# Attention, FFT mixing and FFN in one kernel: one PSUM bank per pair of heads, two in turn, and a new order table

## The chip, the cores and the metric

One core of a Trainium2 chip runs the whole program. The metric is the device time of one execution in microseconds (us); lower is better. TensorE (PE) multiplies, VectorE (DVE) and ScalarE (ACT) do the elementwise work, GpSimd (POOL) very little, and SyncE (SP) issues nearly all transfers.

## The reference

```python
def _attn_ref(q, k, v, cap):                       # (4, 12, 448, 64) each
    scores = np.matmul(q, k.transpose(0, 1, 3, 2)) / np.sqrt(q.shape[-1])
    scores = cap * np.tanh(scores / cap)
    scores = scores - np.max(scores, axis=-1, keepdims=True)
    attn = np.exp(scores)
    attn = attn / (np.sum(attn, axis=-1, keepdims=True) + 1e-09)
    return np.matmul(attn, v)

def _moe_ref(x, w_ch1, w_ch2):                     # x: (4, 448, 768), from attention
    mixed = np.real(np.fft.fft(np.fft.fft(x, axis=1), axis=2))
    u = x + mixed
    un = (u - mean(u)) / np.sqrt(var(u) + 1e-06)   # over the last axis
    return u + np.maximum(un @ w_ch1, 0.0) @ w_ch2 # 768 -> 3072 -> 768
```

## The kernel before

There are 4 batches of 12 heads; the heads go in 24 pairs, six to a batch, and two pairs share one set of q and k tiles. The kernel is a list of small steps. `ORDER` gives each step's place by hand: for each kind of step a list of numbers, by which all steps are sorted (`at`, `plan`). Each engine and the SP queue then run their instructions in that order, one after the other, and wait by semaphores where data or a buffer isn't ready.

For a pair of pairs there are seven *calls* t. `scores(t)` makes 448 queries x 128 rows of scores for two units in PSUM (tag "s", two tiles of two banks), in four 64 x 64 corners of PE. `tanh` moves them to SBUF (five buffers "a") and `exp` works there in place; both are on ACT. `weigh(u)`, two units per call, multiplies the exponentials with v and sums over the keys in PSUM: a pair has seven units, three times two of 128 keys of one head (units 6 or 8 matmuls each) and one of the last 64 keys of both heads. There the two heads lie in the upper and the lower 64 rows of PE, as two row tiles. v carries a column of ones, so one column of each block is the softmax denominator. The accumulator `av` is one tile of two PSUM banks, one bank for each head, and there is one such tile. When a pair's seven units are done, `denominators` and `normalise` on DVE divide and write `u`; the next pair's first matmul into `av` comes after that.

`transform` does the FFT part of a batch, after its six pairs: `fold_tokens`, `mirror`, `fold_features` (DVE), `stage1` (PE, `yps`), `combine` (ACT and DVE), `stage2` (PE, `pq`), `add_u`, `moments`, `rows`, `standardise` (DVE), `u_cols` (PE, `pt`), `u_copy`, `operand` (ACT), `operand_rest` and `residual` (DVE). Weights arrive as 64-bit words and are converted on DVE (`weights`, three steps of nine instructions in all for each half of a weight tile, from `raw` to `w`).

The FFN (`pieces`, step `product`) starts after the last `tanh`: 12 groups, in each for every batch `up` (36 matmuls, `ph`) and `down` (36 matmuls, `po`, each six added to `xc` by DVE at L821). In the first group `down_first` does the first two pieces of a batch with their adds at L845. `down` and `down_first` take their PSUM from tag "av", one tile of two banks (`both`, cut in two), and from tag "d", two tiles of one bank, in turn. Tag "d" also serves `yps`, `pq` and `pt`. From the second group on nothing but the FFN and the conversion of weights is left.

Of the kernel before, what the change touches and what calls it, by code (L numbers as in the profile page):

```python
# [65 lines left out]
PAD = 16, 16  # L66
# [35 lines left out]
        268, 267, 275, 302, 488, 487, 523, 524, 710, 727, 693, 702, 841, 846, 843, 850  # L102
    ],
    "combine": [
        237, 243, 238, 249, 436, 437, 449, 452, 649, 670, 659, 673, 830, 832, 826, 831
    ],
    "denominators": [
        44, 75, 104, 124, 155, 187, 216, 248, 286, 319, 342, 378, 426, 465, 504, 534, 566, 594, 641,
        686, 717, 748, 776, 793
    ],  # L110
    "exp": [
# [5 lines left out]
    ],  # L117
    "fetch": [
        8, 32, 43, 79, 145, 222, 299, 388, 479, 834, 854, 893, 921, 948
    ],  # L120
    "fold_features": [
        214, 228, 210, 223, 415, 419, 395, 407, 629, 637, 627, 634, 813, 815, 809, 811
    ],
    "fold_tokens": [
        149, 168, 186, 164, 196, 194, 261, 287, 367, 336, 382, 386, 498, 592, 554, 557, 607, 608, 698,
        749, 775, 767, 803, 804
# [5 lines left out]
        133, 110, 66, 212  # L132
    ],
    "load_k": [
        0, 28, 50, 37, 91, 106, 128, 161, 177, 245, 258, 264, 315, 376, 372, 438, 494, 477, 515, 581,
        590, 650, 699, 737
    ],
    "load_q": [
        1, 15, 11, 25, 49, 59, 80, 76, 115, 152, 165, 176, 202, 213, 234, 280, 262, 308, 334, 348, 359,
        397, 402, 433, 490, 503, 502, 548, 539, 570, 632, 666, 646, 704, 725, 736  # L140
    ],
    "load_v": [
# [3 lines left out]
    ],  # L146
    "mirror": [
        199, 203, 387, 393, 609, 619, 805, 806
    ],
    "moments": [  # L150
        273, 312, 307, 311, 495, 510, 544, 532, 729, 733, 759, 762, 852, 855, 853, 856
    ],
    "normalise": [
        46, 82, 109, 127, 157, 190, 219, 251, 290, 321, 343, 381, 431, 470, 514, 541, 569, 600, 647,
        690, 722, 751, 777, 798
    ],
    "operand": [
        421, 425, 453, 454, 442, 507, 695, 639, 677, 715, 678, 799, 848, 816, 828, 900, 901, 906, 909,
        923, 916, 907, 920, 927
    ],  # L160
    "operand_rest": [
        458, 430, 486, 469, 456, 537, 720, 652, 680, 723, 763, 833, 886, 822, 887, 902, 910, 911, 912,
        929, 925, 938, 937, 941
    ],
    "product": [
# [3 lines left out]
    ],  # L169
    "residual": [  # L170
        605, 642, 800, 837, 866, 897, 932, 919, 934, 956, 953, 963
    ],
    "row": [
        584, 752, 908, 946
    ],
    "rows": [
        341, 561, 783, 867
    ],
    "rows_cols": [
        346, 564, 794, 875  # L180
    ],
    "rows_copy": [
        355, 598, 795, 880
    ],
    "rows_out": [
        405, 418, 466, 416, 621, 661, 657, 675, 810, 861, 840, 851, 888, 922, 928, 939
    ],
    "scales": [
        4
    ],  # L190
    "scores": [
# [5 lines left out]
    ],  # L197
    "stage1": [
        233, 242, 236, 246, 434, 435, 443, 446, 640, 658, 651, 664, 827, 829, 824, 821
    ],  # L200
    "stage2": [
        259, 254, 269, 291, 473, 472, 505, 511, 709, 716, 684, 687, 838, 845, 839, 849
    ],
    "standardise": [
        363, 354, 347, 368, 567, 576, 583, 580, 790, 789, 791, 786, 876, 879, 883, 874
    ],
    "tanh": [
# [5 lines left out]
    ],  # L213
    "u_cols": [
        374, 375, 391, 392, 409, 414, 599, 597, 616, 620, 628, 633, 796, 802, 814, 808, 862, 869, 884,
        889, 891, 896, 892, 899
    ],
    "u_copy": [
        385, 390, 401, 412, 424, 428, 610, 614, 622, 625, 631, 636, 801, 807, 817, 819, 865, 873, 885,
        890, 895, 898, 904, 905  # L220
    ],
    "warmup": [
        2
    ],
    "weigh": [
# [9 lines left out]
    ],  # L235
    "weights": [
        9, 24, 27, 40, 67, 84, 87, 96, 97, 113, 122, 141, 180, 230, 235, 326, 349, 380, 422, 444, 445,
        556, 586, 648, 663, 689, 825, 872, 878, 894, 915, 930, 940, 944, 947, 950, 959, 962, 964, 966,
        968, 970
    ],  # L240
}


ENGINES = {
    "u_copy": "AAAA",
# [34 lines left out]
def attention_fft_ffn(  # L280
# [60 lines left out]


    vt = new([P, 2, NC, D + 1], F32, "vt", 1, "vt")
    nc.gpsimd.memset(vt[:, :, :, :1], 1.0)

    qk = {}

# [719 lines left out]
```

## Time and profile before

| | before |
|---|---|
| median of 3 runs | 911.3 us (910.24 to 913.85) |
| the profiled execution's own time | 913.63 us |
| its span in the trace | 910.8 us |
| granted TensorE clock | 1.0 |

The span runs from the first to the last instruction that the trace holds; the execution's own time has some 2.8 us more around it. Times in the trace are counted from the span's start. PE shows as busy for 98% of the span, DVE for 80% and ACT for 36%.

### The profile page before, as it was taken

How to read it: one execution, taken by the hardware profiler on the slowest of the kernel's cores; microseconds unless marked ns; L12 is line 12 of the kernel's file. 1: busy time of each engine (PE TensorE's matmuls, PEld its weight loads, DVE VectorE, ACT ScalarE, POOL GpSimd, SP SyncE). 2: the span in 40 equal slices, each digit the busy share in tenths (PEclk: the TensorE clock that was granted, in tenths of full speed). 3: DMA queues.
4: the chain of work that ended last, by engine and by line, in shares of the span. 5: the costliest groups of instructions: out<-in, count | busy, mean ns of one | idle time of the engine just before them, and what ended most of it. 6: DMA issues, size and time to landing. Idle time of an engine off the chain costs nothing.

```text
span 910.8 us, 17992 instructions
## 1 busy us (share of the span) xinstructions
PE 892.0 (98%) x7452; PEld 784.8 (86%) x7452; DVE 728.4 (80%) x1540; ACT 327.1 (36%) x503; POOL 9.7 (1%) x19
## 2 busy tenths in 40 slices
PE   8899999999989999999999999999999999999998
PEld 4566676778889999999999999999999999999998
DVE  4689999999889787878878788787787877878633
ACT  7989999961502212122221221212212221222200
POOL 0000001000000000000000000000000000000000
PEclk9999999999999999999999999999999999999999
DMA  7653535210202121211212211111211111221033
GB/s 212 172 139 104 135 91 164 66 47 1 74 4 84 53 63 55 72 59 53 63 53 63 65 57 53 53 53 53 67 57 53 53 52 53 54 68 53 18 120 123
DMA packets 50465, 66.60 MB, mean 73 GB/s; under 512 B 25408, under 2 KB 36560, under 8 KB 50384
## 3 DMA queue, kind: packets, MB, share of 16 engines
q1 hardware_dynamic: 50096, 65.13, 24.6%
q8 instruction: 58, 0.95, 0.4%
q10 hardware_dynamic: 288, 0.33, 0.1%
q14 instruction: 23, 0.19, 0.1%
HBM read 59.92 MB, written 5.52 MB: 72 GB/s over the span
## 4 chain that ended last, share of the span: by engine, by line
PE 90%; DVE 7%; issue 1%; ACT 1%; POOL 0%; DVEq 0%; POOLq 0%
PE po L813 37%; PE ph L778 37%; PE av L439 7%; PE s L410 6%; PE pq L561 2%; DVE u L477 1%; PE yps L533 1%; DVE xc L768 1%; DVE tf L502 1%; DVE tf L496 1%; DVE ff L515 0%; DVE y L553 0%; PE warm L351 0%; DVE xs L329 0%; PE pt L644 0%
## 5 line engine op out<-in xcount | busy, mean ns | idle before, releaser
L778 PE MATMUL ph<-xs,w 128*128 128x448 f32 x1728 | 353.3, 362 | 0.0
L813 PE MATMUL po<-hh,w 128*128 128x448 f32 (+1 forms) x1686 | 343.7, 362 | 3.6 <-DVE xc L845 3.6
L778 PEld LDWEIGHTS ph<-xs,w 128*128 128x128 f32 x1728 | 323.4, 187 | 21.9 <-issue 0.3
L813 PEld LDWEIGHTS po<-hh,w 128*128 128x128 f32 x1686 | 314.3, 187 | 27.1 <-DVE xc L845 5.1
L821 DVE TENSOR_TENSOR xc<-xc,po 128x448 f32<-128x448 f32 (+1 forms) x281 | 172.2, 616 | 40.3 <-PE po L813 40.2
L790 DVE SCALAR_TENSOR_TENSOR hh<-ph,hh 128x448 fp32r<-128x448 f32 x96 | 59.9, 624 | 87.3 <-ACT hh L789 86.6
L691 ACT ACTIVATE wt<-raw 128x384 f32<-128x384 f32 x84 | 46.6, 555 | 230.5 <-DVE w L725 230.5
L789 ACT ACTIVATE hh<-ph 128x448 fp32r<-128x448 f32 x96 | 52.3, 544 | 187.1 <-PE ph L778 187.1
L439 PEld LDWEIGHTS av<-vt,a 128*64 128x64 f32 (+1 forms) x2688 | 76.7, 137 | 33.7 <-issue 17.2
L439 PE MATMUL av<-vt,a 128*64 128x65 f32 (+1 forms) x2688 | 82.5, 223 | 8.0 <-issue 3.7
L420 ACT ACTIVATE a<-s,tscale 128x896 f32<-128x896 f32 x84 | 82.5, 1005 | 11.8 <-PE s L410 9.7
L324 ACT CAST w<-wt 128x384 fp32r<-128x384 f32 x84 | 42.8, 510 | 117.8 <-DVE wt L700 117.8
L423 ACT ACTIVATE a<-a,capt 128x896 f32<-128x896 f32 x84 | 83.6, 1039 | 0.4
L410 PE MATMUL s<-q,k 64*64 64x448 f32 x672 | 78.5, 560 | 1.5 <-ACT a L420 1.5
L700 DVE SCALAR_TENSOR_TENSOR wt<-wt 128x384 f32<-128x384 f32 x96 | 53.6, 558 | 9.2
L697 DVE SCALAR_TENSOR_TENSOR wt<-raw,wt 128x384 uint32<-128x384 uint32 x96 | 53.7, 559 | 3.3
L725 DVE TENSOR_TENSOR w<-wt 128x384 fp32r<-128x384 f32 x96 | 53.6, 558 | 3.3
L719 DVE SCALAR_TENSOR_TENSOR wt<-raw,wt 128x384 f32<-128x384 uint32 x96 | 53.5, 557 | 2.9
L329 DVE TENSOR_TENSOR wt<-wt,w 128x384 f32<-128x384 f32 x96 | 52.8, 550 | 0.0
L410 PEld LDWEIGHTS s<-q,k 64*64 64x64 f32 x672 | 23.0, 134 | 21.4 <-issue 9.6
L694 DVE TENSOR_SCALAR wt<-raw 128x384 uint32<-128x384 uint32 x96 | 34.1, 355 | 1.1
L716 DVE TENSOR_SCALAR wt<-wt 128x384 uint32<-128x384 uint32 x96 | 33.9, 354 | 0.5
(65 smaller groups left out, 367.7 us busy)
## 6 DMA issues: line engine op xcount, KB each, us to landing
raw<-w2r SPq DMA_DIRECT2D x48, 384.0 KB
raw<-w1r SPq DMA_DIRECT2D x48, 384.0 KB
q<-qr SPq DMA_DIRECT2D x35, 224.5 KB
outT<-xc SPq DMA_DIRECT2D x23, 224.0 KB
k<-kr SPq DMA_DIRECT2D x12, 256.0 KB
vt<-vr SPq DMA_DIRECT2D x24, 128.0 KB
vt<-vr SPq DMA_DIRECT2D x24, 96.0 KB
k<-kr SPq DMA_DIRECT2D x12, 192.0 KB
```

The lines of the kernel that those rows point to most:

```text
L410: nc.tensor.matmul(ps_t[t][h * D : (h + 1) * D, n, :SQ], kt[q, k][rows, k0, h], qk[q, x][rows, :SQ], start=True, stop=True,)
L420: nc.scalar.activation(a_t[t], ps_t.pop(t)[:, :, :SQ], AF.Tanh, scale=tscale)
L423: nc.scalar.activation(a_t[t], a_t[t], AF.Exp, scale=capt)
L439: nc.tensor.matmul(pa_t[p][half * D : (half + 1) * D, j, g * (D + 1) : g * (D + 1) + w], a_t[t][rows, n, q : q + D], vt[rows, p % 2].rearr ...
L697: nc.vector.scalar_tensor_tensor(tu, hi.bitcast(U32), 0xC0000000, tu, op0=ALU.bitwise_and, op1=ALU.bitwise_or)
L700: nc.vector.scalar_tensor_tensor(t, w, HI_MIN, t, op0=ALU.is_ge, op1=mul)
L719: nc.vector.scalar_tensor_tensor(w, lo, 2.0**-52, w, op0=mul, op1=mul)
L725: nc.vector.tensor_tensor(ws[c][1][:, sl], t, w, op=add)
L778: nc.tensor.matmul(ph[:, :S], w_[:, dc * P : (dc + 1) * P], x_, start=(k_ == 0), stop=(k_ == 3 * NDC - 1),)
L790: nc.vector.scalar_tensor_tensor(hh[:, 1], ph[:, :S], 0.0, f32(hh[:, 0]), op0=ALU.max, op1=sub)
L813: nc.tensor.matmul(po[:, q0:q1], w_[:, dc * P : (dc + 1) * P], hh[:, x_, q0:q1], start=(k_ == 0), stop=(k_ == 3 * GF - 1),)
L821: nc.vector.tensor_tensor(ac[:, q0:q1], ac[:, q0:q1], po[:, q0:q1], op=add)
```

## The change

Blocks of 65 columns (64 of v and the column of ones, now the last) of a pair lie side by side in one PSUM bank: three for each head and one for the last 64 queries of both, seven in all. There are two such banks, for even and odd pairs in turn. The last 64 keys of the two pairs that share q and k form the two units in the middle (u = 6 and 7 of 14): unit 6 is the first head of both pairs, unit 7 the second, and each pair has a row tile of its own and writes its own bank. So an even pair ends with unit 7 and an odd pair begins with unit 6. With this the third copy of the queries falls away: two `load_q` in place of three per pair of pairs. `down` and `down_first` take single banks of tag "av" and tag "d" in turn. All lists of `ORDER` are new; the host arrays follow.

```diff
-PAD = 16, 16
+PAD = 24, 16
...
     "denominators": [
-        44, 75, 104, 124, 155, 187, 216, 248, 286, 319, 342, 378, 426, 465, 504, 534, 566, 594, 641,
+        65, 77, 115, 131, 165, 178, 222, 265, 300, 315, 359, 371, 423, 472, 508, 530, 572, 587, 644,
...
-    nc.gpsimd.memset(vt[:, :, :, :1], 1.0)
+    nc.gpsimd.memset(vt[:, :, :, D:], 1.0)
...
-        (nc.scalar if q == 0 and i == 0 else nc.sync).dma_start(qk[q, i], qr[q, i])
+        (nc.scalar if q == 0 and i == 0 else nc.sync).dma_start(qk[q, i], qr[q, i // 2])
...
-        nc.sync.dma_start(vt[:, p % 2, n0:n1, 1:], vr[p // NP, PAIRS[p % NP], :, n0:n1])
+        nc.sync.dma_start(vt[:, p % 2, n0:n1, :D], vr[p // NP, p % NP, :, n0:n1])
...
-                x = (2 * n if n == h else 1) if i == 3 else 2 * (i > 3)
+                x = 2 * (h if i == 3 else i > 3)
...
         p, head, c = chunk(u)
-        if u % NC == 0:
-            pa_t[p] = psum.tile([P, 2, 512], F32, tag="av", bufs=1, name="av")
-        i = 6 if head is None else 2 * c + head
-        first, last = ((0, 1), (6, 6)) if p % 2 == 0 else ((0, 0), (6, 6))
-
-        def tile(j, g, half, rows, n, i):
+        if u % (2 * NC) in (0, NC - 1):
+            pa_t[u // NC + (u % NC > 0)] = psum.tile([P, 512], F32, tag="av", name="av")
+
+        def tile(p, j, g, half, rows, n, i, start):
+            block = 3 * j + g if g < 3 else 6
             q = (2 * g + half) * D if g < 3 else 6 * D
-            w = D + 1 + int(g == 2 and c == 0 and half != j)
             nc.tensor.matmul(
-                pa_t[p][half * D : (half + 1) * D, j, g * (D + 1) : g * (D + 1) + w],
+                pa_t[p][half * D : (half + 1) * D, block * (D + 1) : (block + 1) * (D + 1)],
                 a_t[t][rows, n, q : q + D],
-                vt[rows, p % 2].rearrange("k n c -> k (n c)")[:, i * (D + 1) : i * (D + 1) + w],
-                start=u % NC == first[j] and g == 0,
-                stop=u % NC == last[j] and g == 3,
+                vt[rows, n if i == NC - 1 else p % 2, i],
+                start=start,
+                stop=False,
                 skip_group_check=True,
             )
 
+        if head is None:
+            p -= p % 2
+            for g in range(3):
+                for h in range(2):
+                    for half in range(2):
+                        tile(p + h, n, g, half, slice(h * D, (h + 1) * D), n, NC - 1, h == 1 and n == g == 0)
+            if n == 1:
+                for j in range(2):
+                    for h in range(2):
+                        tile(p + h, j, 3, j, slice(h * D, (h + 1) * D), j, NC - 1, False)
+            return
         for g in range(3):
-            for j in (0, 1) if head is None else (head,):
-                rows = slice(P) if head is not None else slice(j * D, (j + 1) * D)
-                for half in range(2):
-                    tile(j, g, half, rows, n, i)
-        for j in range(2):
-            if head is None:
-                tile(j, 3, j, slice(j * D, (j + 1) * D), n, i)
-            elif head == 1:
-                tile(j, 3, j, slice(P), n - 1 + j, i - 1 + j)
+            for half in range(2):
+                tile(p, head, g, half, slice(P), n, 2 * c + head, u % (2 * NC) == g == 0)
+        if head == 1:
+            for j in range(2):
+                tile(p, j, 3, j, slice(P), n - 1 + j, 2 * c + j, False)
...
-        pa = pa_t[p][:, :, : 4 * (D + 1)].rearrange("q j (g c) -> q j g c", g=4)
-        den = den_t[p] = new([P, 2, 4, 1], F32, "den", 2, "den")
-        nc.vector.tensor_scalar_add(den, pa[:, :, :, :1], guard)
+        pa = pa_t[p][:, : 7 * (D + 1)].rearrange("q (i c) -> q i c", i=7)
+        den = den_t[p] = new([P, 7, 1], F32, "den", 2, "den")
+        nc.vector.tensor_scalar_add(den, pa[:, :, D:], guard)
...
-        def part(out, rows, j, g):
-            x = pa[rows, j, g]
-            nc.vector.tensor_tensor(out, x, den[rows, j, g].to_broadcast(x.shape), op=mul)
-
-        part(u[D:FOLD, :, 3], slice(FOLD, P), slice(2), 2)
-        nc.vector.memset(den[FOLD:, :, 2], 0.0)
+        def part(out, rows, i):
+            x = pa[rows, i]
+            nc.vector.tensor_tensor(out, x, den[rows, i].to_broadcast(x.shape), op=mul)
+
+        part(u[D:FOLD, :, 3], slice(FOLD, P), slice(2, 6, 3))
+        nc.vector.memset(den[FOLD:, 2:6:3], 0.0)
         for j in range(2):
-            part(u[:D, j, 3], slice(j * D, (j + 1) * D), j, 3)
-        part(u[:, :, :3], slice(P), slice(2), slice(3))
+            part(u[:D, j, 3], slice(j * D, (j + 1) * D), 6)
+        nc.vector.tensor_tensor(
+            u[:, :, :3],
+            pa[:, :6].rearrange("q (j g) c -> q j g c", j=2),
+            den[:, :6].rearrange("q (j g) c -> q j g c", j=2).to_broadcast([P, 2, 3, D]),
+            op=mul,
+        )
...
-        both = yield from down_first(b) if g == 0 else ()
+        if g == 0:
+            yield from down_first(b)
         for dc in range(2 * (g == 0), NDC):
 
-            if dc % 2:
-                po = psum.tile([P, 512], F32, tag="d", name="po")
-            else:
-                if dc % 4 == 0:
-                    both = psum.tile([P, 2, 512], F32, tag="av", bufs=1, name="po")
-                po = both[:, dc % 4 // 2]
+            po = psum.tile([P, 512], F32, tag=("av", "d")[dc % 2], name="po")
...
-        both = psum.tile([P, 2, 512], F32, tag="av", bufs=1, name="po")
-        po = both[:, 0], psum.tile([P, 512], F32, tag="d", name="po")
+        po = [psum.tile([P, 512], F32, tag=tag, name="po") for tag in ("av", "d")]
...
-            at(load_v, p, i, needs=[("weigh", u) for u in units(p - 2)])
+            at(load_v, p, i, needs=[("weigh", 7 * p - 8 + n) for n in range(2 - p % 2)] if p > 1 else [])
...
-                at(denominators, p, needs=[("weigh", 7 * p + 6), ("guards",)] + ([("denominators", p - 1)] if p else []))
+                at(denominators, p, needs=[("weigh", 7 * p + 7 - p % 2), ("guards",)] + ([("denominators", p - 1)] if p else []))
```

How the order moves instructions is shown at three places. First VectorE, the rows up to the first denominators (`den`; `w` and `wt` are a converted weight and its scratch). Before:

```order
L725 TENSOR_TENSOR w_177<-wt 128x384
L693 TENSOR_SCALAR wt<-raw 128x384
L694 TENSOR_SCALAR wt<-raw 128x384
L697 SCALAR_TENSOR_TENSOR wt<-raw,wt 128x384
L700 SCALAR_TENSOR_TENSOR wt<-wt 128x384
L466 TENSOR_SCALAR den<-av,guard 128x8
L467 RECIPROCAL den<-den 128x8
```

After:

```order
L735 TENSOR_TENSOR w_193<-wt 128x384
L703 TENSOR_SCALAR wt<-raw 128x384
L704 TENSOR_SCALAR wt<-raw 128x384
L707 SCALAR_TENSOR_TENSOR wt<-raw,wt 128x384
L710 SCALAR_TENSOR_TENSOR wt<-wt 128x384
L726 TENSOR_SCALAR wt<-wt 128x384
L326 CAST w_308<-wt 128x384
L729 SCALAR_TENSOR_TENSOR wt<-raw,wt 128x384
L471 TENSOR_SCALAR den<-av,guard 128x7
L472 RECIPROCAL den<-den 128x7
```

The first denominators now stand behind the third conversion's first seven instructions, 12 conversion instructions later than before.

Second TensorE, at the change from the second pair to the third (`av` with its number is the accumulator, `a` the exponentials, `s` the scores). Before:

```order
L439 MATMUL av_284<-vt_92,a_273 64x65 x8
L410 MATMUL s_383<-q_323,k_219 64x448 x4
L410 MATMUL s_392<-q_323,k_219 64x448 x4
L439 MATMUL av_402<-vt_92,a_313 64x65 x5
L439 MATMUL av_402<-vt_92,a_313 64x66
L439 MATMUL av_402<-vt_92,a_313 64x65 x4
```

After:

```order
L437 MATMUL av_259<-vt_92,a_246 64x65 x14
L437 MATMUL av_259<-vt_92,a_244 64x65 x14
L437 MATMUL av_385<-vt_92,a_325 64x65 x14
L410 MATMUL s_405<-q_220,k_323 64x448 x4
L437 MATMUL av_385<-vt_92,a_321 64x65 x14
L410 MATMUL s_430<-q_220,k_323 64x448 x4
```

Before, the third pair's tile `av_402` starts behind two calls of scores; now its bank `av_385` follows the second pair's last unit directly. The shared units stand earlier, as alternating rows of `av_157` and `av_259`:

```order
L410 MATMUL s_248<-q_169,k_222 64x448 x4
L437 MATMUL av_157<-vt_92,a_167 64x65 x2
L437 MATMUL av_259<-vt_92,a_167 64x65 x2
L437 MATMUL av_157<-vt_92,a_167 64x65 x2
L437 MATMUL av_259<-vt_92,a_167 64x65 x2
```

Third TensorE, in the first FFN group, from `down_first` of a late batch to the third and fourth piece of the same `down` (`po` with its number is the PSUM tile). Before:

```order
L836 MATMUL po_3787<-hh_3745,w2_177 128x448 x3
L836 MATMUL po_3788<-hh_3745,w2_177 128x448 x3
L836 MATMUL po_3787<-hh_3783,w2_452 128x448 x3
L836 MATMUL po_3788<-hh_3783,w2_452 128x448 x3
L813 MATMUL po_3787<-hh_3745,w2_177 128x448 x3
L813 MATMUL po_3787<-hh_3783,w2_452 128x448 x3
L813 MATMUL po_3817<-hh_3745,w2_177 128x448 x3
L813 MATMUL po_3817<-hh_3783,w2_452 128x448 x3
```

After:

```order
L841 MATMUL po_3751<-hh_3718,w2_193 128x448 x3
L841 MATMUL po_3752<-hh_3718,w2_193 128x448 x3
L841 MATMUL po_3751<-hh_3745,w2_308 128x448 x3
L841 MATMUL po_3752<-hh_3745,w2_308 128x448 x3
L819 MATMUL po_3782<-hh_3718,w2_193 128x448 x3
L819 MATMUL po_3782<-hh_3745,w2_308 128x448 x3
L819 MATMUL po_3792<-hh_3718,w2_193 128x448 x3
L819 MATMUL po_3792<-hh_3745,w2_308 128x448 x3
```

Before, the third piece goes into the second bank of the tile whose first bank took the first piece (`po_3787`); now it has a bank of its own (`po_3782`). In the changed order the first `yps` of batch 0 stands behind 28 calls of `scores` and 406 matmuls of `weigh` (7.25 pairs), where it stood behind 30 calls and 426 (7.61 pairs); for batch 1 it is 48 calls and 692 (12.36 pairs) against 50 and 728 (13).

## Rows read from the trace of the kernel before

**Rows 1.** The page: span, and busy time, share and instructions of PE.

```profile
span 910.8 us, 17992 instructions
PE 892.0 (98%) x7452; PEld 784.8 (86%) x7452; DVE 728.4 (80%) x1540; ACT 327.1 (36%) x503; POOL 9.7 (1%) x19
```

**Rows 2.** Windows: stretch, busy us and instructions by engine, clock, DMA share, GB/s.

```profile
7.30:62.00 54.70, 49.22 (x1016) 29.75 (x1008) 35.49 (x99) 50.31 (x55) 0.00 (x0) 1.00 0.63 173
62.00:196.00 134.00, 129.50 (x2777) 92.57 (x2774) 126.79 (x336) 122.12 (x149) 6.22 (x8) 1.00 0.37 102
196.00:275.00 79.00, 75.37 (x478) 66.42 (x477) 73.35 (x151) 22.90 (x44) 1.27 (x2) 1.00 0.12 37
275.00:910.80 635.80, 632.78 (x3168) 592.22 (x3166) 491.10 (x947) 130.09 (x253) 0.00 (x0) 1.00 0.20 61
```

**Rows 3.** Chain that ended last, in time order: start us, us, what.

```profile
113.89 1.95 PE yps L533 x32
...
118.29 1.66 PE s L410 x16
119.95 2.12 PE pq L561 x32
...
145.39 3.32 PE av L439 x112
...
237.20 2.32 PE pt L644 x24
```

**Rows 4.** Timeline at the first and last change of pair: start, us, what.

```profile
17.47 1.04 DVE L477 TENSOR_TENSOR u<-av,den 64x64 f32<-64x64 f32 x3
...
18.62 0.59 PE L439 MATMUL av<-vt,a 64*64 64x65 f32 x25 [0.54 <-PE s L410]
...
191.59 1.04 DVE L477 TENSOR_TENSOR u<-av,den 64x64 f32<-64x64 f32 x3
...
192.74 0.65 PE L439 MATMUL av<-vt,a 64*64 64x65 f32 x27 [1.38 <-issue]
```

**Rows 5.** Waits of DVE, 7 to 62 and 62 to 200: us, times, longest.

```profile
DVE den L466 <- PE av L439: 16.7, 6, 5.6
...
DVE y L553 <- ACT yh L324: 0.9, 1, 0.9
DVE den L466 <- PE av L439: 0.7, 3, 0.4
```

**Rows 6.** Waits of ACT, 7.3 to 62 us.

```profile
ACT a L420 <- PE s L410: 5.7, 5, 1.6
```

**Rows 7.** Waits of PE from 196 us on, and the timeline at the third wait.

```profile
PE po L813 <- DVE xc L845: 3.6, 4, 1.4
...
250.33 2.08 DVE L768 TENSOR_TENSOR xc<-xc,dev 128x896 f32<-128x896 f32 x2
252.33 1.14 DVE L845 TENSOR_TENSOR xc<-xc,po 128x448 f32<-128x448 f32 x2
...
253.00 1.28 PE L813 MATMUL po<-hh,w 128*128 128x448 f32 x5 [1.43 <-DVE xc L845]
```

**Rows 8.** Timeline of DVE: first and last of the nine instructions of a conversion.

```profile
6.46 0.36 DVE L693 TENSOR_SCALAR wt<-raw 128x384 uint32<-128x384 uint32 x1 [0.58 <-DMA raw<-w2r]
...
9.91 0.56 DVE L725 TENSOR_TENSOR w<-wt 128x384 fp32r<-128x384 f32 x1
```

**Rows 9.** Timeline of DVE: denominators of the eighth and the last pair.

```profile
69.46 0.23 DVE L466 TENSOR_SCALAR den<-av,guard 128x8 f32<-128x8 f32 x1
...
196.08 0.23 DVE L466 TENSOR_SCALAR den<-av,guard 128x8 f32<-128x8 f32 x1
```

**Rows 10.** Groups of DVE by form, 0 to 200 us: busy us, mean ns, idle before.

```profile
L585 DVE TENSOR_TENSOR u<-u,pq 128x384 f32<-128x384 f32 x24 | 11.7, 547 | 0.1
```

**Rows 11.** Timeline at the first `yps` of batch 0.

```profile
63.36 0.63 DVE L515 TENSOR_TENSOR ff<-tf 128x194 f32<-128x194 f32 x2
...
64.21 1.92 PE L533 MATMUL yps<-seqT,ff 128*64 128x128 f32 x32
```

More of the change, by code (lines that the diff above doesn't have):

```diff
@@ L131 @@
     "load_constant": [
-        133, 110, 66, 212
+        197, 148, 47, 185
     ],
     "load_k": [
-        0, 28, 50, 37, 91, 106, 128, 161, 177, 245, 258, 264, 315, 376, 372, 438, 494, 477, 515, 581,
-        590, 650, 699, 737
+        1, 16, 37, 59, 73, 71, 128, 174, 204, 216, 278, 277, 283, 377, 416, 417, 464, 498, 507, 519,
+        564, 608, 697, 731
     ],
     "load_q": [
-        1, 15, 11, 25, 49, 59, 80, 76, 115, 152, 165, 176, 202, 213, 234, 280, 262, 308, 334, 348, 359,
-        397, 402, 433, 490, 503, 502, 548, 539, 570, 632, 666, 646, 704, 725, 736
+        2, 11, 23, 36, 93, 124, 157, 146, 191, 232, 257, 295, 308, 361, 395, 459, 490, 492, 542, 586,
@@ L155 @@
-        690, 722, 751, 777, 798
+        72, 91, 121, 141, 177, 181, 246, 268, 306, 318, 370, 374, 429, 480, 520, 532, 583, 591, 657,
+        703, 741, 758, 786, 791
     ],
     "operand": [
-        421, 425, 453, 454, 442, 507, 695, 639, 677, 715, 678, 799, 848, 816, 828, 900, 901, 906, 909,
-        923, 916, 907, 920, 927
+        441, 489, 390, 458, 457, 408, 601, 624, 626, 675, 637, 800, 797, 877, 813, 886, 890, 894, 891,
+        893, 902, 919, 918, 912
     ],
     "operand_rest": [
-        458, 430, 486, 469, 456, 537, 720, 652, 680, 723, 763, 833, 886, 822, 887, 902, 910, 911, 912,
@@ L163 @@
-        929, 925, 938, 937, 941
+        531, 588, 559, 593, 539, 411, 667, 690, 816, 743, 824, 811, 868, 879, 829, 888, 892, 896, 914,
+        916, 917, 926, 925, 930
     ],
     "product": [
[3 rows of a table removed]
[3 rows of a table added]
     ],
     "residual": [
-        605, 642, 800, 837, 866, 897, 932, 919, 934, 956, 953, 963
+        640, 668, 642, 771, 858, 882, 898, 905, 921, 941, 949, 953
     ],
     "row": [
-        584, 752, 908, 946
+        578, 654, 867, 935
     ],
     "rows": [
-        341, 561, 783, 867
+        319, 533, 746, 847
@@ L178 @@
     ],
     "rows_cols": [
-        346, 564, 794, 875
+        347, 548, 761, 863
     ],
     "rows_copy": [
-        355, 598, 795, 880
+        360, 550, 776, 866
     ],
     "rows_out": [
-        405, 418, 466, 416, 621, 661, 657, 675, 810, 861, 840, 851, 888, 922, 928, 939
+        387, 406, 528, 476, 561, 615, 584, 605, 789, 790, 857, 820, 872, 933, 911, 899
     ],
     "scales": [
-        4
+        3
     ],
     "scores": [
[5 rows of a table removed]
[5 rows of a table added]
     ],
     "stage1": [
-        233, 242, 236, 246, 434, 435, 443, 446, 640, 658, 651, 664, 827, 829, 824, 821
+        219, 230, 224, 237, 407, 403, 428, 433, 645, 656, 639, 661, 815, 814, 817, 819
@@ L216 @@
-        889, 891, 896, 892, 899
+        362, 363, 368, 378, 384, 397, 582, 585, 606, 627, 611, 635, 767, 794, 805, 803, 826, 856, 870,
+        874, 878, 876, 880, 885
     ],
     "u_copy": [
-        385, 390, 401, 412, 424, 428, 610, 614, 622, 625, 631, 636, 801, 807, 817, 819, 865, 873, 885,
-        890, 895, 898, 904, 905
+        367, 369, 382, 386, 389, 401, 590, 609, 623, 628, 631, 643, 774, 801, 810, 812, 831, 859, 871,
+        875, 883, 884, 895, 897
     ],
     "warmup": [
-        2
+        0
@@ L846, in down_first @@
             yield
-        return both
     def pieces():
@@ L899, in prepare @@
         for i in range(2):
-            at(load_v, p, i, needs=[("weigh", u) for u in units(p - 2)])
+            at(load_v, p, i, needs=[("weigh", 7 * p - 8 + n) for n in range(2 - p % 2)] if p > 1 else [])
             if p % 2 == 0:
-                for x in (0,) if i == 0 else (1, 2):
-                    t0, t1 = ((0, 4), (3, 4), (3, 7))[x]
+                x = 2 * i
+                if 1:
+                    t0, t1 = ((0, 4), (), (3, 7))[x]
                     at(load_q, p // 2, x, needs=[("scores", 7 * (p // 2 - 1) + t) for t in range(t0, t1)] if p else [])
@@ L909, in attend @@
         pairs = sorted({u // 7 for u in (2 * t, 2 * t + 1)})
-        at(scores, t, needs=[("load_q", t // NC, x) for x in ((0, 1, 2) if t % NC == 3 else (2 * (t % NC > 3),))] + [("load_k", t // NC, int(t % NC >= KT[1]))])
+        at(scores, t, needs=[("load_q", t // NC, x) for x in ((0, 2) if t % NC == 3 else (2 * (t % NC > 3),))] + [("load_k", t // NC, int(t % NC >= KT[1]))])
         at(tanh, t, needs=[("scores", t), ("scales",)])
@@ L1036 @@
     for j in range(2):
-        kr[..., 3, j * D : (j + 1) * D] = kj[:, :, j, :, 3 * P :]
+        kr[..., 3, j * D : (j + 1) * D] = kj[:, j, ..., 3 * P :]
+    vj = v.reshape(B, NP, 2, S, D)[:, PAIRS]
     vr = np.empty((B, NP, P, NC, D), np.float32)
     for j in range(2):
-        vr[:, :, :, j:6:2] = v[:, j::2, : 3 * P].reshape(B, NP, 3, P, D).transpose(0, 1, 3, 2, 4)
-        vr[:, :, j * D : (j + 1) * D, 6] = v[:, j::2, 3 * P :]
+        vr[:, :, :, j:6:2] = vj[:, :, j, : 3 * P].reshape(B, NP, 3, P, D).transpose(0, 1, 3, 2, 4)
+        vr[:, j::2, :, 6] = vj[:, :, j, 3 * P :].reshape(B, NP // 2, P, D)
     arrays = {
         "qr": np.concatenate(
-            [qr.reshape(B * NP // 2, 3, P, SQ), np.broadcast_to(np.float32(cap), (B * NP // 2, 3, P, 1))], axis=3
+            [qj.reshape(B * NP // 2, 2, P, SQ), np.broadcast_to(np.float32(cap), (B * NP // 2, 2, P, 1))], axis=3
         ),
```

34 lines of the change are left out of this document (16 added, 18 removed), and 60 rows, old and new, of the table ORDER.

## The prediction, on record before the changed kernel ran

> **What bounds the kernel now.** I read the stretches first, then the chain of waits, then single places. The page has PE busy for 892 us of a span of 910.8 [rows 1]. By stretch the kernel falls in two [rows 2]: from 275 us on there are 3168 matmuls in 635.8 us, 0.2007 us each, with no gap, so nothing the change does can shorten that part; it can only start sooner. Before 275 us PE is also nearly always marked busy, but a marked PE is not a full one, so I rebuilt its work from back-to-back groups [rows 3]: 16 score matmuls take 1.66 us (0.83 us for one call of `scores`), a pair's 112 `weigh` matmuls 3.32, 32 `yps` 1.95, 32 `pq` 2.12, 24 `pt` 2.32. Up to the last `weigh` at 196.0 us that is 84 x 0.83 + 24 x 3.32 + 6 x 1.95 + 6 x 2.12 + 2 x 2.32 = 178.4 us. The scores begin at 5.5 us, so 190.5 us were available and **12.1 us of PE were lost** in the attention part.
>
> Where: at the change of pair. The one accumulator tile is read by `normalise`, and the next pair's first matmul follows it. At the first change `normalise` ends at 17.47 + 1.04 = 18.51 and PE starts at 18.62; at the last it ends at 192.63 and PE starts at 192.74 after 1.38 us idle [rows 4]. Of the 23 changes 17 look like this (start within 0.26 us of the end of `normalise`); at the other six PE had enough other work in front.
>
> The loss has a second side. DVE stood 16.7 us before 62 us with a denominator at the head of its queue, waiting for PE; from 62 to 200 us it waited 0.7 us for that and 0.9 us for ACT [rows 5] and was busy 126.8 of 134.0 us [rows 2]. So DVE idles early and sets the pace later: the early idle is what could pay for the later part. ACT waited 5.7 us for scores between 7.3 and 62 us [rows 6]; its busy time from 7.3 to 196 us is 50.3 + 122.1 = 172.4 us [rows 2], so it could not end the attention before about 180 us. The granted clock is 1.00 in every stretch [rows 2].
>
> After 196 us PE waits at four places only, 3.6 us together, all at L813 for the add of L845 [rows 7]. There `down` wants the second half of the two-bank tile while the add still reads the first half: DVE does two `residual` steps at 250.33 and the add at 252.33, and PE starts at 253.00.
>
> **The change, part by part.**
>
> *One bank per pair, two in turn.* Removes the wait of rows 4: a pair's bank is wanted again only a pair or so later. What follows depends on who is late next. PE alone would allow up to 12.1 us, ACT more. DVE is the tightest from 62 us on, and there I count. From the denominators at 69.46 us (the eighth pair) to those at 196.08 (the last) DVE took 126.6 us with next to no wait [rows 9]. In the changed order one weight conversion more stands ahead of the eighth pair's denominators, and four `add_u` instructions and two smaller ones of the transform; the first denominators alone have 12 more conversion instructions in front of them, as the order shows. A conversion's nine instructions run from 6.46 to 9.91 + 0.56 = 10.47, 4.0 us [rows 8]; four `add_u` at 0.55 us are 2.2 [rows 10], the two smaller ones, less than that each, some 0.8: 7.0 us leave this stretch. Against this, two `residual` steps (2.08 us for two, rows 7), one small copy (0.3) and two fewer `operand_rest` (0.6 each by the size of an `add_u` or a little more) put 1.2 us net into it. So 126.6 - 7.0 + 1.2 = 120.8 us: **5.8 us less**. The 7.0 us now lie where DVE waited 16.7, so I take them as hidden; if that cover were gone the eighth pair would come 7.0 us later and the term would be -1.2 or nothing. At the other end, if the early changes of pair also fall away, the eighth pair comes sooner as well, by at most the 5.7 us that ACT waited there, and the sum is then held by PE at 12.1. Bounds: 0 and -12.1; I take -5.8, the one row in which a single engine ran without a wait.
>
> *The last 64 keys of two pairs in one unit.* The unit has 14 matmuls as before, twice per pair of pairs, on 64 rows in two row tiles that write different banks, as they did. The 112 matmuls of a pair stay 112; the 66-wide ones become 65 wide, one column in 66 of a few per pair. Even pairs end one unit later, odd ones begin one unit sooner. Nothing. The divisions read 7 blocks in place of 8; the large one has 384 elements either way. Nothing.
>
> *Two query loads.* 12 loads of some 0.22 MB go, where the transfer engines were busy 0.63 and 0.37 of the time [rows 2] and no wait of PE or ACT for such a load stands in the trace after the start. Nothing; and with four buffers the next group's queries can be asked for sooner, which covers a load that the new order places late.
>
> *`down` in single banks.* The third piece of each batch in the first group takes the other bank, so it needs no add. Its fourth uses tag "d", its fifth the first bank again: by then PE has done two pieces, 12 x 0.2 = 2.4 us after the last matmul of `down_first`, where DVE was some 1.5 us late at 253 us. So the 3.6 us go. At other places DVE may now be late; in the new order of the last batch's transform I find the waits and the work in front of them equal within some 0.3 us at two places and charge **0.5 us**. Bounds: -3.6 and 0. After 275 us PE had no wait to lose.
>
> Sum: -5.8 - 3.6 + 0.5 = -8.9 us. The profiled execution took 913.6 us (2.8 us outside its span), so it would be 904.7; the median of the runs shown is 911.3, 2.3 lower, and I predict against that: **902.4 us**.
>
> **The rivals.**
>
> A. *The bank was not the bound.* PE had scores to do at each change, so another engine keeps the pace and only the term of `down` remains: 911.3 - 3.1 = 908.2. For it: DVE is 95% busy from 62 us on. Against it: PE starting 0.1 us after `normalise` at so many changes, and DVE waiting for PE in its turn early on. The Trainium skill, page "TensorE: Matmul & The Clock Gate", section "HAM oscillation — how this bites in real kernels", tells of a kernel in which double-buffering PSUM gave no further gain. By that rule this rival would be the result; rows 4 speak against it, since there the bank is what was waited for.
>
> B. *The add of L845 stays in the way*, because DVE has the same work in less time after an earlier end of the attention: 911.3 - 5.8 = 905.5. For it: DVE was busy 73.35 of 79.0 us between 196 and 275 [rows 2].
>
> C. *All early waits go too*, and PE runs nearly full: 911.3 - 12.1 - 3.1 = 896.1. Against it: ACT needs 172 of 189 us there and shares two score buffers with PE.
>
> D. *Slower: PE parks at the transform.* The changed order puts the first `yps` of batch 0 behind 28 calls of `scores` and 7.25 pairs; before it was 30 and 7.61. So PE comes there 2 x 0.83 + 0.36 x 3.32 = 2.9 us of its work sooner. Before, the last fold ended at 63.99 us and `yps` began at 64.21 [rows 11]: there is no slack. If DVE, with 12 more instructions ahead of its first denominators, isn't sooner by as much, PE stands, the scores behind it come late, and ACT with them: 2.9 us plus the 0.6 us by which DVE's work ahead of the fold grew. For batch 1 the same count (48 and 12.36 against 50 and 13) gives 1.7 + 2.1 = 3.8. With nothing won at the pairs that is 911.3 + 7.3 - 3.1 = 915.5, without `down` 918.6. It decides at the fold of batch 0: DVE must get from the sixth pair's denominators to there in 8 us, not the 10.8 it took. Against it: seven instructions of a `normalise` that stood between have gone behind the folds.
>
> **How the numbers follow.** Forecast (both terms, 898.5 to 906.5): 0.52. A 0.18, B 0.11, C 0.13, D 0.06. The likeliest is the forecast, 902.4. The range must leave out no more than 2 in 10: it takes in B, most of A and of C: 897 to 909.5. What a measurement of this kernel can tell from no change is about 0.5%, 4.6 us, so faster means under 906.7. Faster: nearly all of the forecast and C, two thirds of B, a little of A: 0.74. Within: most of A, a third of B, D where its parking is short: 0.20. Slower, from 915.9: 0.06.
>
> **What would show it.** In the profile after: no start of a pair's first matmul tied to the end of a `normalise`; DVE's wait for denominators before 62 us down from 16.7 to some 10 us or less; the last denominators at about 190 us, not 196; no wait of L813's counterpart for an add; the matmuls from there on at 0.2007 us each, so that the end moves by what the first 275 us save. It is wrong if DVE's early wait stays (then D or A), if PE stands at `yps`, if the clock granted falls, or if one `weigh` matmul costs more than its 3.32 / 112 = 0.030 us with a pair's matmuls all in one bank.

## The result, and the profile after

The changed kernel takes **899.7 us** (median of 4 executions, 897.77 to 901.64) beside 911.3 us for the kernel before: a ratio of 0.9869 [0.9833, 0.9904], 11.6 us faster where 8.9 were predicted. Run a second time, beside its own runs of the kernel before (911.5 us), it took 898.9 us (897.86 to 899.16), 0.9859 [0.9843, 0.9875]. The profiled execution of the first time took 901.64 us, with a span of 899.9.

The page after, beside [rows 1]:

```profile
span 899.9 us, 17955 instructions
PE 890.4 (99%) x7452; PEld 784.9 (87%) x7452; DVE 727.4 (81%) x1540; ACT 325.8 (36%) x503; POOL 9.0 (1%) x19
```

The work is the same to within 2 us on every engine. What went is for the most part time in which PE stood: 18.8 us of the span were not busy on PE before, 9.5 are now. By windows, beside [rows 2] (stretch, busy us and instructions of PE, PEld, DVE, ACT and POOL, granted clock, DMA share, GB/s):

```profile
7.30:62.00 54.70, 51.30 (x1084) 31.75 (x1078) 40.83 (x112) 51.44 (x57) 0.00 (x0) 0.97 0.56 161
62.00:185.00 123.00, 122.76 (x2542) 84.90 (x2538) 116.85 (x311) 115.56 (x144) 5.49 (x8) 1.00 0.37 101
185.00:264.00 79.00, 78.54 (x647) 71.73 (x643) 75.49 (x164) 27.12 (x49) 1.26 (x2) 1.00 0.09 27
264.00:899.90 635.90, 632.74 (x3168) 592.70 (x3166) 493.19 (x950) 130.03 (x254) 0.00 (x0) 1.00 0.20 61
```

The last 3168 matmuls take 635.9 us as before (635.8), so the whole gain lies ahead of them. In the first stretch PE does 68 matmuls more in the same 54.7 us and DVE 13 instructions more, and there alone the granted clock is below 1.00 (0.97; more on that below). The waits of PE for another engine's work in the whole span (us, times, longest) are now these. Beside them the view has only 2.2 us at the warm-up, as before, and 0.3 us with no releaser:

```profile
PE s L410 <- ACT a L420: 2.5, 3, 1.9
PE av L437 <- ACT a L423: 0.5, 1, 0.5
PE pq L571 <- DVE y L563: 0.4, 1, 0.4
```

No matmul of a pair waits for a `normalise` [rows 4], and the 3.6 us at the add of L845 [rows 7] are gone. DVE's waits from 7 to 62 us, and from 62 to 190 us, beside [rows 5]:

```profile
DVE den L471 <- PE av L437: 11.7, 6, 3.5
...
DVE den L471 <- PE av L437: 0.8, 1, 0.8
```

The denominators of the eighth and of the last pair, beside [rows 9], in the execution profiled first and then in the one of the second run:

```profile
70.25 0.22 DVE L471 TENSOR_SCALAR den<-av,guard 128x7 f32<-128x7 f32 x1
...
190.98 0.23 DVE L471 TENSOR_SCALAR den<-av,guard 128x7 f32<-128x7 f32 x1
```

```profile
66.22 0.22 DVE L471 TENSOR_SCALAR den<-av,guard 128x7 f32<-128x7 f32 x1
...
187.23 0.23 DVE L471 TENSOR_SCALAR den<-av,guard 128x7 f32<-128x7 f32 x1
```

The stretch between the two is 120.7 and 121.0 us; it was 126.6, and the prediction said 120.8. But the eighth pair, which the prediction left at 69.46 us, came at 70.25 in one execution and at 66.22 in the other. Of these 4.0 us, 1.4 were there already at the fourth pair's denominators (36.11 and 34.74 us); where those come from stays open. Most of the rest happened at 42 us. There PE (start, us, what) stood for 1.95 us ahead of the first scores of the fourth pair of pairs:

```profile
41.11 1.04 PE L437 MATMUL av<-vt,a 128*64 128x65 f32 x28
44.09 0.98 PE L410 MATMUL s<-q,k 64*64 64x448 f32 x8 [1.95 <-ACT a L420]
```

The trace puts this down to a tanh of L420. The last one ahead of the matmul ran from 42.33 to 43.32 us, as the timeline of ACT says, and had ended 0.77 us before, so something else was waited for:

```profile
42.33 0.99 ACT L420 ACTIVATE a<-s,tscale 128x896 f32<-128x896 f32 x1
```

What came later is most likely a load. SP's timeline and, from the view of the transfers, what was moved from 42 to 46 us in slices of 0.1 us:

```profile
36.54 1.94 SPq L391 DMA_DIRECT2D q<-qr  x1
38.53 0.42 SPq L376 DMA_DIRECT2D seqT<-seq  x1
39.06 0.39 SPq L687 DMA_DIRECT2D raw<-w1r  x1
39.48 0.43 SPq L391 DMA_DIRECT2D q<-qr  x1
```

```profile
GB/s 369 369 374 300 272 236 192 187 133 161 54 72 54 36 54 54 18 0 0 0 0 0 0 0 0 0 0 0 0 0 0 0 0 0 0 164 0 0 0 0
```

The scores of call 21 need the query load that was issued last, at 39.48 us; transfers go on until 43.7, and PE starts at 44.09. Why it is late can be read in the table of the order: the fourth group's second query load has number 146, its first one, which is needed first, 157, and a load of `seqT` (148) and a weight fetch (155) stand between. After this stand the granted clock fell (windows, columns as above):

```profile
42.00:44.00 2.00, 0.14 (x6) 0.00 (x1) 1.07 (x3) 2.00 (x3) 0.00 (x0) 1.00 0.39 147
44.00:46.00 2.00, 1.91 (x57) 1.55 (x61) 0.00 (x0) 2.00 (x3) 0.00 (x0) 0.76 0.03 8
46.00:48.00 2.00, 2.00 (x29) 0.60 (x24) 1.30 (x5) 1.01 (x2) 0.00 (x0) 0.50 0.18 40
48.00:50.00 2.00, 2.00 (x63) 2.00 (x64) 1.04 (x4) 1.94 (x2) 0.00 (x0) 0.89 1.00 232
```

By the three lower means PE lost (0.24 + 0.50 + 0.11) x 2.0 = 1.7 us more. Of the four executions two had a mean clock of 0.998 (901.64 and 901.47 us) and two of 1.000 (897.88 and 897.77): 3.7 us apart. The second run's four all had 1.000; in its trace the load was issued at 37.62 us, and PE stood 0.86 us:

```profile
41.65 0.98 PE L410 MATMUL s<-q,k 64*64 64x448 f32 x8 [0.86 <-ACT a L423]
```

So the longer stand and the lower clock are 1.95 - 0.86 + 1.7 = 2.8 us of the 4.0 between the two traces.

### The profile page after: what moved, and what is told of

It reads as the page before. It is cut to its first block, busy times and chain, and to the rows that moved or that the text cites. A ratio compares the mean times of both kernels' runs of the same rounds, so it can differ in the third digit from the quotient of the medians.

```text
span 899.9 us, 17955 instructions
## 1 busy us (share of the span) xinstructions
PE 890.4 (99%) x7452; PEld 784.9 (87%) x7452; DVE 727.4 (81%) x1540; ACT 325.8 (36%) x503; POOL 9.0 (1%) x19
## 4 chain that ended last, share of the span: by engine, by line
PE 92%; ACT 4%; DVE 3%; issue 0%; POOL 0%; POOLq 0%; DVEq 0%; ACTq 0%
PE ph L788 38%; PE po L819 37%; PE av L437 6%; PE s L410 6%; PE pq L571 2%; ACT a L420 2%; ACT a L423 2%; PE po L841 1%; PE yps L543 1%; DVE y L563 1%; PE pt L654 1%; DVE tf L512 0%; PE warm L351 0%; DVE tf L506 0%; DVE ff L525 0%
## 5 line engine op out<-in xcount | busy, mean ns | idle before, releaser
L420 ACT ACTIVATE a<-s,tscale 128x896 f32<-128x896 f32 x84 | 82.3, 1010 | 8.9 <-PE s L410 7.4
L410 PEld LDWEIGHTS s<-q,k 64*64 64x64 f32 x672 | 20.7, 135 | 22.2 <-ACT a L420 9.3
## 6 DMA issues: line engine op xcount, KB each, us to landing
q<-qr SPq DMA_DIRECT2D x23, 224.5 KB
```

The source lines that it names most:

```text
L410: nc.tensor.matmul(ps_t[t][h * D : (h + 1) * D, n, :SQ], kt[q, k][rows, k0, h], qk[q, x][rows, :SQ], start=True, stop=True,)
L420: nc.scalar.activation(a_t[t], ps_t.pop(t)[:, :, :SQ], AF.Tanh, scale=tscale)
```

## The experiments

Three groups, each beside its own runs of the kernel before (911.33, 910.94 and 911.54 us); the three groups ran on three chips. First: what the late load costs, and what the parts of the change are worth alone.

**The two query loads of the fourth group exchanged** (changed kernel, `load_q`):

```
-        2, 11, 23, 36, 93, 124, 157, 146, 191, ...
+        2, 11, 23, 36, 93, 124, 146, 157, 191, ...
```

> The changed kernel with two numbers of its order exchanged, so that on SP's queue the first query load of the fourth group goes ahead of the second one and of a table and a weight load. Theory (the late load stops PE for 1.95 us at 42.1 us, and the clock falls to half after it for 3.4 us in some executions): PE's gap there goes, the granted clock is 1.00 in every stretch and every execution, and the time is 896 to 897.5 us in all, 1.0 to 2.5 us under the 897.8 of the executions whose clock did not fall. Rival (ACT sets the pace there and PE would have to stand anyway): the gap stays or moves by a few us, and the time stays spread over 897.8 to 901.6.

Measured: 898.50 us (897.64 to 899.29), 0.9855 [0.984, 0.987], mean clock 0.999 to 1.000 in all four. PE's stand at the first scores of that group is gone. It starts them at 41.92 us, right behind the work before:

```profile
40.95 1.04 PE L437 MATMUL av<-vt,a 128*64 128x65 f32 x28
41.92 0.98 PE L410 MATMUL s<-q,k 64*64 64x448 f32 x8
```

Two numbers of an order table, exchanged, remove the stand that the trace had put down to ACT, and it is absent from five later traces with the exchange too, so it was the load. The time is another matter: 896 to 897.5 us were expected, below the executions whose clock had not fallen, and weren't reached. DVE's early wait fell to 7.8 us, the stretch between the denominators stayed at 120.7 us (67.1 to 187.8). The changed kernel's two executions with a clock of 0.998 lie 3 us above it, the others level with it.

**Useless matmuls where PE stood** (changed kernel, in `scores`, into the transform's tag):

```
+        if t == 21:
+            fill = psum.tile([P, 512], F32, tag="d", name="fill")
+            for _ in range(4):
+                nc.tensor.matmul(fill[:, :P], ident, ident, start=True, stop=True)
```

> The changed kernel with four matmuls without use (1.9 us by the 0.48 us that one of the warm-up takes) put on PE in front of the scores that wait for the late query load; the load stays late. If the fall of the clock comes from PE standing still there, the clock stays 1.00 in every execution and the time is 897.8 in all; the load still ends the wait. If the clock falls for another reason, executions of about 901.5 with 0.998 remain. If neither gap nor clock counts because ACT is the bound, no change in either value.

Measured: 899.21 us (897.94 to 899.48), 0.986 [0.9845, 0.9875], clock 1.000 in all four; 897.8 was expected in all.

```profile
42.10 1.16 PE L408 MATMUL fill<-ident 128*128 128x128 f32 x8
43.19 0.98 PE L414 MATMUL s<-q,k 64*64 64x448 f32 x8
```

The filling took 1.16 us, and the scores follow without a gap. The clock did not fall. That fits a fall that follows a longer stand, but in this trace the load was there sooner as well, and the changed kernel by itself had executions without a fall, so it doesn't prove it.

**`down` alone** (kernel before; the third piece of each batch in the first group takes a bank of tag "ph", where the changed kernel gives it the other bank of tag "av"):

```
+            elif g == 0 and dc == 2:
+                po = stage["up"].tile([P, 512], F32, tag="ph", name="po")
```

> The kernel before with one edit: the third piece of each batch in the first group of the FFN takes a bank of tag ph, not the second half of the tile that the first piece's add still reads. Theory: the four waits of 3.6 us go, 907.7 us (ratio 0.996). Rival (VectorE is late there and the wait only moves on to the next piece): 910 to 911.3, with a wait of PE for an add at another piece.

Measured: 907.88 us (6 executions, 906.01 to 908.98), 0.9953 [0.9938, 0.9968]: 3.4 us. In its trace the waits for the add are gone and nothing came for them; DVE's early wait is 16.3 us as before. From the last denominators (195.5 us) to the end (906.1) are 710.6 us, where the kernel before took 910.8 - 196.08 = 714.7: **4.1 us**.

**The changed tiles in the old order** (changed kernel with the tables of before, the middle one of each three query loads dropped, the first unit behind the seventh of each even pair put right after it, since the two share the last 64 keys):

```
+ORDER["load_q"] = [x for i, x in enumerate(ORDER["load_q"]) if i % 3 != 1]
+for _p in range(0, B * NP, 2):
+    ORDER["weigh"][7 * _p + 7] = ORDER["weigh"][7 * _p + 6] + 0.1
+    ORDER["load_v"][2 * _p + 3] = min(ORDER["load_v"][2 * _p + 3], ORDER["weigh"][7 * _p + 6] - 0.1)
```

> The changed kernel's tiles, units and loads with the order numbers of the kernel before (unit 8 of each pair of pairs moved up behind unit 7, a few v loads earlier for it, the third query loads dropped). The waits of PE for a bank fall away here too, VectorE's queue is as before. Theory of the forecast (VectorE sets the pace from 62 us on and only the shift of its work into the early part helps): the attention part gains 0 to 1 us, 906.5 to 907.7 with the gain in down. Rival (the wait for the bank itself was the loss): the attention part gains 5 us or more, 899 to 902.5.

Measured: 901.92 us (901.45 to 902.32), 0.9892 [0.9878, 0.9907]. This is the run that corrects the prediction most.

```profile
63.75 0.23 DVE L476 TENSOR_SCALAR den<-av,guard 128x7 f32<-128x7 f32 x1
...
189.56 0.22 DVE L476 TENSOR_SCALAR den<-av,guard 128x7 f32<-128x7 f32 x1
```

The rival held: with the old order the stretch keeps its length (125.8 us, 126.6 before), and the two banks give their time **ahead** of it. The eighth pair comes 69.46 - 63.75 = 5.7 us sooner, and ACT's waits for scores there are down from 5.7 us to 1.2. From the last denominators to the end are 710.2 us, as with `down` alone. So of 9.4 us, some 3.4 are `down` and 6.0 the banks (together with the shared unit and the loads, which weren't tried apart in this order), and the new order adds some 3.

How much of that lies in the stretch can be read by counting PE's work in it, here for the old order and for the new one with the exchanged loads (groups of instructions between the two denominators: instructions, busy us, mean ns, idle time ahead and what ended it):

```profile
L415 PE MATMUL s<-q,k 64*64 64x448 f32 x432 | 47.9, 548 | 1.1 <-ACT a L425 1.0
L576 PE MATMUL pq<-featT,y 97*64 97x192 f32 (+1 forms) x192 | 13.5, 289 | 0.1
L548 PE MATMUL yps<-seqT,ff 128*64 128x128 f32 (+5 forms) x128 | 8.0, 274 | 1.9 <-DVE y L568 1.9
```

```profile
L410 PE MATMUL s<-q,k 64*64 64x448 f32 x412 | 46.8, 549 | 0.0
L571 PE MATMUL pq<-featT,y 97*64 97x97 f32 (+1 forms) x176 | 13.0, 290 | 0.2 <-DVE y L563 0.2
```

The new order has moved 20 score matmuls and 16 `pq` ahead of the eighth pair: 2.1 + 1.1 us by the prediction's rates. So the eighth pair comes later than in the old order (67.08 us against 63.75) and the stretch is shorter (120.7 against 125.8), and much of the one pays for the other. What is won up to the last denominators is 189.56 - 187.81 = 1.7 us: PE's stands in the stretch, 3.7 us in the old order (the 1.9 for `y` among them), are 0.2 in the new one.

Second: which engine sets the pace between 66 and 190 us. All three below have the exchanged query loads as their base (898.5 us).

**More DVE work inside the stretch** (eight `bn_stats` of batches 0 and 1 said twice):

```
+            for _ in range(2 if b in (0, 1) and i == 0 else 1):
                 nc.vector.bn_stats(bs[:, i, :], u[:, i * 384 : (i + 1) * 384])
```

> The kernel with the exchanged query loads (898.5 us, last denominators at 187.8 us) and 8 statistics instructions of VectorE said twice between 73 and 155 us (0.5 us each, 4.0 us more of its work). Theory of the forecast (VectorE sets the pace from the eighth pair on): eighth to last denominators 124 to 125 us in place of 120.7, the time 901.5 to 902.5. Rival (TensorE is full there by now and VectorE only follows): 0 to 1 us more, 898.5 to 899.5.

Measured: 901.05 us (900.71 to 901.48), 0.989 [0.9874, 0.9907]: 2.6 us more than the base for 20.3 - 15.8 = 4.5 us of added DVE work (40 instructions in place of 32). The base ran on another chip; beside the kernel with DVE work added early (898.80, below, on this one) it is 2.3 us. The stretch is 124.1 us, 3.4 longer:

```profile
66.46 0.22 DVE L471 TENSOR_SCALAR den<-av,guard 128x7 f32<-128x7 f32 x1
...
190.58 0.23 DVE L471 TENSOR_SCALAR den<-av,guard 128x7 f32<-128x7 f32 x1
```

**More PE work inside the stretch** (a useless matmul ahead of each second stage of batches 0 and 1, eight in all):

```
+        if b in (0, 1):
+            nc.tensor.matmul(ps[:, :P], ident, ident, start=True, stop=True)
```

> The kernel with the exchanged query loads and 8 matmuls without use, one ahead of each second transform stage of the first two batches (0.48 us each by the warm-up, 3.8 us more of TensorE's work between 65 and 125 us). Theory of the forecast (VectorE sets the pace): 0 to 1 us more, 898.5 to 899.5. Rival (TensorE is full): 901.5 to 902.5. If both this and the kernel with more VectorE work come out some 4 us longer, the two engines are level and neither has cover left.

Measured: 901.65 us (901.46 to 902.53), 0.9899 [0.9884, 0.9914]: 3.2 us more. One useless matmul is two instructions here, and the next work starts 0.42 us after it:

```profile
63.59 0.49 PE L568 MATMUL pq<-ident 128*128 128x128 f32 x2
64.01 1.20 PE L573 MATMUL pq<-featT,y 97*64 97x192 f32 x16
```

Eight of them are 3.4 us, and nearly all of it is paid; the stretch is 123.7 us. So PE has next to no cover in the stretch (3.2 of 3.4 us are paid, 2.9 beside the run on the same chip), and DVE has little (2.6 or 2.3 of 4.5). "DVE is the tightest" was half of it: in the changed kernel the two are nearly level, PE the tighter. That neither can win much more alone is likely but wasn't tried.

**More DVE work ahead of the stretch** (12 more instructions of 0.36 us in the first six conversions):

```
+                early.append(s)
+                for _ in range(3 if len(early) <= 6 else 1):
                     nc.vector.tensor_scalar(w.bitcast(U32), hi.bitcast(U32), 0x7FFFFFFF, None, op0=ALU.bitwise_and)
```

> The kernel with the exchanged query loads and 12 instructions of VectorE more in the first six weight conversions (0.36 us each, 4 us more of its work ahead of the eighth pair; it waits 7.8 us there for denominators). Theory of the forecast (what lies ahead of the eighth pair is hidden by that wait): 0 to 0.5 us more, 898.5 to 899. Rival (only part of the early wait can be used, as the kernel with the old order suggests, whose eighth pair came at 63.8 us against 67.1 with 7.0 us less of this work ahead of it): 1.5 to 2.5 us more, 900 to 901.

Measured: 898.80 us (897.77 to 899.03), 0.9864 [0.9849, 0.9878]: 0.3 us more, no change that can be told. The 4.3 us (12 x 0.36) came out of DVE's early wait, which fell from the first row (exchanged loads) to the second (this run):

```profile
DVE den L471 <- PE av L437: 7.8, 6, 2.7
```

```profile
DVE den L471 <- PE av L437: 4.3, 4, 1.9
```

Third: what a third query load per group costs, and the changed kernel once more.

**A second load into the same tile** (exchanged loads as base; this one ran with the second group):

```
+        if i == 2:
+            nc.sync.dma_start(qk[q, i], qr[q, i // 2])
```

> The kernel with the exchanged query loads and the second query load of each pair of pairs issued twice, so that as many loads and bytes as in the kernel before are on the queue. Theory of the forecast (the twelve loads are hidden): 898.5, within 1 us. Rival (the queue and the transfers are on the path early on): some loads come late again, 900 us or more, with a stop of TensorE for one of them in the trace.

Measured: 907.38 us (905.96 to 908.68), 0.996 [0.9945, 0.9975], mean clock 0.996 to 0.998: 8.9 us more. It doesn't answer the question it was made for. The second load writes the tile that the first is still writing, so SP holds it back until the first has landed, and all loads behind it too (SP's waits, 0 to 190 us):

```profile
SPq L393 <- DMA q<-qr: 39.0, 12, 5.2
```

**A third load into a tile of its own**, 160 KB (a dropped load was 224.5 KB):

```
+        if i == 2:
+            nc.sync.dma_start(new([P, 320], F32, "qx", 1, "qx"), qr[q, 1][:, :320])
```

> The kernel with the exchanged query loads and a third load of 160 KB for each pair of pairs, right behind the second one, into a small tile of its own that nothing reads, so that SP does not stand for a load that has to land in the same tile first (in the kernel that issued the load twice SP stood 39 us for that). Theory (the loads that went were hidden): 898.5, within 1 us, so that the 8.9 us of that kernel came from the queue standing. Rival (the loads themselves count, where the early transfers are at 0.55 of what they can do): 901 us or more.

Measured: 897.83 us (897.25 to 898.46), 0.9846 [0.9832, 0.9861]: no dearer than its base, so twelve more loads of this size cost nothing that can be told. The loss of the run before goes with SP's standing; how much of it is the lower clock wasn't separated.

**The changed kernel again**, and **the exchanged loads again**, with the run above:

> The changed kernel again, without an edit, on one chip with the next. If the late query load and the fall of the clock after it are what spread its times, executions of about 898 us at a granted clock of 1.000 and of about 901.5 at 0.998 come again, some of each. If the spread was chance, one value with 1.000.

> The kernel with the exchanged query loads again, on one chip with the changed kernel. Theory: 1.000 in every execution, 897.5 to 899.5, and 1 to 3 us under the median of the changed kernel. Rival (the exchange does nothing that a measurement can tell): equal medians and the same spread.

Measured: 898.91 us (897.86 to 899.16), 0.9859 [0.9843, 0.9875], and 898.39 us (898.09 to 898.94), 0.9853 [0.9838, 0.9868]. The difference of 0.5 us can't be told from none, and no execution of about 901.5 us came again: of the two outcomes named, it is the one by which the first spread was chance. The exchange removes PE's stand at 42 us, but that it makes the kernel faster, or keeps the clock up, isn't shown: its eight executions all had a clock of 0.999 or more, and so had six of the changed kernel's eight.

## Why the prediction was right

The time lay in its range, and both terms of the forecast came: the waits on the accumulator and on the add are gone. But the larger term came for another reason than the one counted, so that its size came out near is in part luck. By its own steps:

- **What bounds the kernel.** Right: the waits on the accumulator are gone, and so is their time. The Trainium skill, page "TensorE: Matmul & The Clock Gate", section "HAM oscillation — how this bites in real kernels", reports no further gain from double-buffering PSUM in its kernel. Here the new tiles in the old order measured 6.0 us beyond `down`, so for this kernel, where DVE reads the one accumulator between two pairs [rows 4], that report doesn't hold.
- **The bank's term, -5.8 us.** Two things held: the stretch took 120.7 and 121.0 us where 120.8 were counted, and DVE's work ahead of it is hidden (4.3 us more of it cost 0.3). What failed is the step from there to the gain, "DVE is the tightest from 62 us on, and there I count". By it the banks in the old order would have gained next to nothing (0 to 1 us, as was expected of that run), and they gained 6.0 us, nearly all ahead of the stretch. The sum had left the eighth pair at 69.46 us and named its coming sooner "by at most the 5.7 us that ACT waited there" as a bound only; it came 5.7 us sooner. Up to the last denominators the term measured **-8.9 us** in the second run's trace (196.08 - 187.23 = 8.85) and -5.1 in the one profiled first; with the old order it was -6.5 (196.08 - 189.56).
- **The count of 120.8 us for the stretch.** It came true, but it can't be told from PE's: the PE work of the new order in the stretch, by the rates of [rows 3], is 53.1 + 42.7 + 11.7 + 7.8 + 5.0 = 120.3 us (1792 `weigh`, 412 score, 176 `pq`, 128 `yps` and 52 `pt` matmuls), with 0.2 us of waits; in the old order it is 123.3. So PE's moved work shortens the stretch as well as DVE's, and what each gives wasn't tried apart.
- **`down`, -3.6 us.** 4.1 us in the trace and 3.4 in the median with this part alone.
- **The charge of 0.5 us for DVE late in the last transform.** About right in size: PE waits 0.4 us for DVE there, at one `pq` at 204 us. Even so, from the last denominators to the end the changed kernel takes 708.9 us, 5.8 less than before where 3.1 were predicted, and 1.3 to 1.7 less than `down` alone or the old order. Which move of the new order gives this rest wasn't tried and stays open. (8.9 and 5.8 are more than the 11.6 or 12.6 us of the medians, since the profiled execution before was 2.3 us above its median.)
- **The half unit: nothing.** 56 matmuls take 67.03 - 65.40 = 1.63 us after, 0.029 us each (0.030 before), so the matmuls are no dearer.

```profile
65.40 1.81 PE L437 MATMUL av<-vt,a 128*64 128x65 f32 x56
67.03 1.17 PE L571 MATMUL pq<-featT,y 97*64 97x192 f32 x16
```

- **Two query loads: nothing, and "covers a load that the new order places late".** The first half fits the third load in a tile of its own, though that was 160 KB and not the whole. The second was wrong at one place: the order of the two loads of the fourth group was itself turned round, and no sentence of the prediction looked at it. The late load made PE stand 1.95 us in the execution profiled first, where 1.7 us were lost by the clock after it, and 0.86 us in the second run's trace. That this moves the median isn't shown.
- **Rivals.** A (908.2) and B (905.5) fell with the waits of PE; D fell because PE has no wait at `yps`. C (896.1) was half right: the early waits went in part, from 16.7 to 11.7 or 7.6 us, and the time ended between the forecast and C, about as near to the one as to the other.
- **What would show it.** All held, save one in the execution profiled first: DVE's early wait there was 11.7 us, not 10 or less; that execution had the long stand. Of what would make it wrong, one thing came: the granted clock fell in two executions. They were 3.7 us slower than the other two, too little to leave the range.

## What to carry to other kernels

When one accumulator is read between two groups of matmuls, a second bank can be worth the stands that end with that read: here the banks, with the shared unit and the loads that went with them, gave some 6 us and the order some 3 more. Work of an engine costs little where it waits anyway, and must be paid where it is full: 4.3 us of DVE's work added ahead of the eighth pair cost 0.3 us, 4.5 added behind it 2.6. Don't take the length of a stretch between two marks for a gain before you have counted what every engine does in it, since a new order moves the marks too. After a change of order, check for each operand that the loads are issued in the order in which they are used, and don't take a releaser's name in the trace for the cause where that instruction had ended long before.

## What the runs showed that was not expected

- A stand of 1.95 us (with 0.14 us of PE work in 2 us) was followed by three slices of 2 us at granted clocks of 0.76, 0.50 (1.2 GHz) and 0.89, in an execution that else had 1.00; after a stand of 0.86 us at the same place, in another execution, the clock stayed at 1.00.
- A second transfer into a tile that a first one is still filling made SP's queue stand for 39.0 us in 12 waits, 3.3 us each, and the kernel took 8.9 us more, while an extra transfer of 160 KB into another tile, also 12 times, cost nothing that can be told.
- The same useless matmul (two instructions) took 1.16 / 4 = 0.29 us in a run of four and 0.42 us alone between other work.
